# First batch of an attention + Fourier mixing + feed-forward kernel: mirrored columns folded by matmuls, sum and difference accumulated on TensorE, last value products in two steps

## The chip, the cores and the metric

One core of one Trainium2 chip. The metric is the device time of one execution in microseconds (us). The kernel before took 617.75 us, the median of three runs from 617.31 to 617.80. Every variant was timed in five rounds against the kernel before on the same chip.

## The reference

Eight batches, each of 448 positions and 12 heads of 64, hence 768 features.

```python
q_n = q / (norm(q) + 1e-6);  k_n = k / (norm(k) + 1e-6)
attn = softmax(q_n @ k_n.T / tau)
x = concat_heads(attn @ v)                        # [8, 448, 768]
u = x + real(fft(fft(x, axis=1), axis=2))         # mixing over positions, then features
un = (u - mean(u)) / sqrt(var(u) + 1e-6)
out = u + relu(un @ w_ch1) @ w_ch2                # 768 -> 3072 -> 768
```

The kernel does the real part of the two-dimensional transform as cosine and sine tables multiplied on TensorE. Symmetry halves the work: rows k and -k share the products P = C X C and Q = S X S, and one output is P + Q, its mirror P - Q.

## The kernel before

A small scheduler in Python orders the instructions of five engines by estimated durations and priorities; the order it finds is fixed in the program. So any change to batch 0 also reorders what comes after. The parts that matter:

```python
# filler matmuls, put in to keep TensorE's clock up in the head (cut)
n = int(0.75 * (op.start - t - 0.1) / 0.036)
if bank and n > 0:
    new = Op(("pe",), make(bank[0], n), (0.036 * n,), 0, "warm")
# the 24 weight pieces, all on GpSimd's queue; each waits for the piece three before it
for i in range(24):
    ...
    prev.append(P.add("pool", fn, 0.8, 9, nm, writes=[nm], dma=(nm, 16), after=[prev[-3]], serve=2.1))
self.w = prev[3:]
# loads of q and k: those of the third batch (b == 2) wait for the 8th piece of the second matrix
gate = [self.w[19]] if b == 2 else []
# loads of v, also on GpSimd's queue: those of the second batch wait for the 12th piece of the first
gate = [self.loads[3]] if b == 0 else [self.w[11]] if b == 1 else []
# fold: mirrored columns added and subtracted on VectorE into G, then the sequence step fs
return v.tensor_tensor(gp(G[:], ...), gp(F[:], ...), gp(F[:], [[fs_, 2], [384, 2], [-1, n]], ...), o)
...
r = pe.matmul(o, G[0:k, eo, 2 * s + t, ...], self.CSs[0:k, t, s, :], start=(t == 0), stop=(t == 1))
# feature step fd: the cosine product into one bank, the sine product into the next
r = pe.matmul(PS[:, bk + s, m0:m1], self.Tt[0:k, o0:o0 + 128], self.CSd[0:k, d, s, m0:m1], ...)
# ScalarE copies one product out; VectorE makes sum and difference; then the adds into U
P.add("act", lambda a, ...: a.activation(SN[2], PS[:, bank + 1, 0:NL], ACTF.Copy), ...)
for sg, o in ((0, AluOp.add), (1, AluOp.subtract)):
    P.add("dve", lambda v, ...: v.tensor_tensor(SN[sg], PS[:, bank, 0:NL], SN[2], o), ...)
```

## Time and profile before

| | kernel before |
|---|---|
| time, median of 3 | 617.75 us |
| span of the profiled run | 616.0 us |
| TensorE busy | 591.1 us, 96% |
| GpSimd busy | 96.3 us, 16% |
| first feed-forward matmul (line 1000) | 55.96 us |
| first matmul of the second layer (line 1022) | 103.29 us |

Up to 55.96 us is the "head", in which the first batch's attention and transform run while TensorE has nothing of its own to do. From 103.29 us to the end TensorE is busy for 507.4 of 512.7 us. The prediction shows the windows, the chain of waits and GpSimd's timeline.

### The profile page before, as it was taken

Reading aid. Unit: us, or ns where it says so; the run is one execution under the profiler, and the core shown is the slowest. Engines: PE = TensorE matmul, PEld = TensorE weight load, DVE = VectorE, ACT = ScalarE, POOL = GpSimd, SP = SyncE. Lnnn points to the kernel's source line nnn. Section 1 sums busy time; section 2 is a strip of 40 time slices with the busy share of each in tenths; the row PEclk is TensorE's granted clock in tenths of the full one; section 3 lists DMA queues with packets and bytes.
Section 4 is the critical chain, followed back from the end, with each engine's and each line's share of the span. In section 5 each row is a group of like instructions: output and inputs, shape, how many; then the busy total and the mean of one; then the engine's idle time right before and its main releaser. Section 6 shows DMA issues by size and latency. Waiting matters only on the chain.

```text
span 616.0 us, 13590 instructions
## 1 busy us (share of the span) xinstructions
PE 591.1 (96%) x5604; PEld 384.7 (62%) x5621; DVE 389.0 (63%) x896; ACT 346.5 (56%) x690; POOL 96.3 (16%) x125
## 2 busy tenths in 40 slices
PE   4788999999999999999999999999999999999998
PEld 3567777667866666655566676566556766654464
DVE  7887987797778677877788669667643670010011
ACT  7784797247873688347745856685576125104300
POOL 8721512010004102010030130003000010010010
PEclk8899999999999999999999999999999999999999
DMA  7999998889339536973196393716720140010001
GB/s 186 120 213 217 159 181 115 95 153 183 76 72 189 122 78 94 131 168 78 30 142 132 95 173 67 162 53 104 58 40 2 53 102 1 27 39 13 1 27 77
DMA packets 187629, 62.02 MB, mean 101 GB/s; under 512 B 166704, under 2 KB 185264, under 8 KB 187568
## 3 DMA queue, kind: packets, MB, share of 16 engines
q1 hardware_dynamic: 129648, 38.35, 32.4%
q0 software_dynamic: 57920, 22.81, 28.8%
q8 instruction: 44, 0.72, 0.5%
q14 instruction: 17, 0.14, 0.1%
HBM read 51.90 MB, written 11.01 MB: 102 GB/s over the span
## 4 chain that ended last, share of the span: by engine, by line
PE 87%; DVE 6%; ACT 2%; POOL 2%; issue 2%; DMA 1%; POOLq 0%; DVEq 0%; ACTq 0%
PE PS L1000 34%; PE PS L1022 34%; PE PS L782 5%; PE PS L751 5%; PE PS L779 2%; PE PS L847 2%; PE PS L882 2%; ACT E L733 2%; DVE U L903 1%; DMA VB<-in_v_dram 1%; DVE ST L930 1%; PE PS L763 1%; PE PS L764 1%; PE PS L1097 1%; DVE OUTB L1031 0%
## 5 line engine op out<-in xcount | busy, mean ns | idle before, releaser
L1000 PE MATMUL PS<-UNT,W1b 128*128 128x256 bf16 (+3 forms) x1424 | 230.6, 315 | 3.4 <-issue 1.3
L1022 PE MATMUL PS<-W2b,hT 128*128 128x384 bf16 (+2 forms) x1343 | 229.7, 326 | 0.1
L1000 PEld LDWEIGHTS PS<-UNT,W1b 128*128 128x128 bf16 x1440 | 129.2, 98 | 87.2 <-ACT hT L1009 3.0
L1022 PEld LDWEIGHTS PS<-W2b,hT 128*128 128x128 bf16 x1344 | 128.8, 98 | 81.9 <-issue 2.6
L733 ACT ACTIVATE E<-PS 128x900 bf16<-128x900 f32 (+1 forms) x192 | 150.0, 826 | 42.6 <-PE PS L751 35.1
L1009 ACT ACTIVATE hT<-PS 128x384 bf16<-128x384 f32 (+3 forms) x170 | 81.0, 477 | 94.7 <-PE PS L1000 93.2
L1031 DVE TENSOR_TENSOR OUTB<-PS,U 128x384 f32<-128x384 f32 (+2 forms) x56 | 31.2, 557 | 116.1 <-PE PS L1022 115.2
L1052 POOL DMA_INDIRECT out_dram<-OUTB,IDX x20 | 22.0, 1099 | 328.2 <-DVE OUTB L1031 188.8
L668 DVE TENSOR_REDUCE SS<-QH 128x6 f32<-128x384 f32 x84 | 45.4, 541 | 14.0 <-ACT QH L666 13.8
L1010 DVE TENSOR_SCALAR hT<-PS 128x256 bf16<-128x256 f32 (+3 forms) x70 | 35.3, 505 | 27.6 <-PE PS L1000 26.4
L782 PE MATMUL PS<-VB,E 128*128 128x65 bf16 x1152 | 51.2, 193 | 0.0
L782 PEld LDWEIGHTS PS<-VB,E 128*128 128x128 bf16 x1152 | 47.7, 97 | 1.7
L666 ACT ACTIVATE QH<-STG 128x384 f32<-128x384 f32 x84 | 43.6, 519 | 7.2 <-DVE SS L668 4.3
L713 POOL DMA_DIRECT2D VB<-in_v_dram x24 | 25.3, 1063 | 128.7 <-PE PS L782 127.8
L751 PE MATMUL PS<-QT,KT 64*128 64x225 bf16 x576 | 43.1, 262 | 2.0 <-ACT E L733 1.7
L779 PE MATMUL PS<-VZ,E 128*128 128x130 bf16 x192 | 42.3, 220 | 1.5 <-DMA VB<-in_v_dram 1.2
L903 DVE TENSOR_TENSOR U<-SQT,X 128x384 bf16<-128x384 f32 (+3 forms) x80 | 40.8, 551 | 0.8
L675 DVE TENSOR_TENSOR QH<-STG,RN 128x768 bf16<-128x768 f32 x42 | 39.7, 950 | 0.5
L796 DVE TENSOR_TENSOR X<-PS,RD 128x512 bf16<-128x512 f32 x48 | 33.2, 691 | 1.5
L751 PEld LDWEIGHTS PS<-QT,KT 64*128 64x128 bf16 x576 | 21.3, 94 | 20.0 <-ACT E L733 8.7
L794 DVE RECIPROCAL RD<-PS 128x8 f32<-128x8 f32 x48 | 9.9, 206 | 32.2 <-PE PS L782 32.0
L857 ACT ACTIVATE Tt<-PS 128x900 bf16<-128x900 f32 (+2 forms) x15 | 13.4, 893 | 28.1 <-PE PS L847 28.1
(117 smaller groups left out, 485.4 us busy)
## 6 DMA issues: line engine op xcount, KB each, us to landing
STG<-in_q_dram SPq DMA_DIRECT2D x18, 384.0 KB, 5.0
STG<-in_k_dram SPq DMA_DIRECT2D x18, 384.0 KB, 4.0
VB<-in_v_dram POOLq DMA_DIRECT2D x24, 192.0 KB, 6.3
W1b<-in_moe_w_ch_dram POOLq DMA_DIRECT2D x12, 384.0 KB, 8.2
W2b<-in_moe_w_ch_dram POOLq DMA_DIRECT2D x12, 384.0 KB, 6.2
out_dram<-OUTB SPq DMA_DIRECT2D x7, 384.0 KB, 2.4
hT<-in_k_dram SPq DMA_DIRECT2D x2, 576.0 KB, 5.4
hT<-in_q_dram SPq DMA_DIRECT2D x2, 576.0 KB, 6.9
```

The costliest lines, as they stand in the source:

```text
L666: P.add("act", lambda a, sq=sq, src=buf[:, w * x:w * x + w]: a.activation(sq, src, ACTF.Square), t_act(w), pr, f"sq{i}_{b}", reads=bn, wri ...
L668: P.add("dve", lambda v, o=SS[:, i, H // ns * x:H // ns * (x + 1)], sq=sq: v.tensor_reduce(o, sq.rearrange("p (h d) -> p h d", d=DH), AX.X ...
L675: P.add("dve", lambda v, i=i, buf=buf, qh=qh: v.tensor_tensor(v3(qh), v3(buf), RN[:, i, :].unsqueeze(2).to_broadcast((128, H, DH)), AluOp. ...
L733: return a.activation(o, self.PS[:, bk:bk + nc_, 0:SQ2], ACTF.Exp, scale=1.0 / self.tau)
L751: i = pe.matmul(self.PS[:, bk + h, c0:c0 + NK], self.KT[r, jj, kt * 128:(kt + 1) * 128], self.QT[r, jj, cols], start=True, stop=True)
L779: pe.matmul(o, st(6), self.VZ[:, j, :], start=True, stop=False, skip_group_check=True)
L782: r = pe.matmul(o[:, 65 * h:65 * h + 65], st(2 * kt + h), self.VB[:, kt, 2 * j + h, :], start=False, stop=(h == 1 and kt == 2), skip_group ...
L903: return v.tensor_tensor(U[o0:o0 + n, ut, cs].rearrange("p (i e) -> p i e", e=2), src, X[i0:i0 + n, x, cs].rearrange("p (i e) -> p i e", e ...
L1000: r = pe.matmul(self.PS[:, bk, 0:n], self.W1b[:, j, ft * 128:(ft + 1) * 128], unT[:, j, cs], start=(j == 0), stop=(j == NJ - 1))
L1009: return e.activation(self.hT[:, ft, cs], self.PS[:, bk, 0:n], ACTF.Relu)
L1010: return e.tensor_relu(self.hT[:, ft, cs], self.PS[:, bk, 0:n])
L1022: r = pe.matmul(self.PS[:, bk, 0:n], self.hT[:, ft, 128 * i:128 * i + 128], self.W2b[:, ft, c0:c0 + n], start=(ft == 0), stop=(ft == NF - 1))
```

## The change

The intent is to shorten the head. Four things are done to batch 0 only: the last head pair's value products run in two steps; mirrored columns of the first of two blocks are no longer folded on VectorE but multiplied against a mirrored table, as twice as many matmuls (with that, the copy of this block's result, Tt, goes to ScalarE alone); P + Q and P - Q are accumulated on TensorE, the latter with a negated sine table; and fillers come as 8 per 0.6 us in place of one long block. Two negated tables are made by two new GpSimd instructions.

```diff
@@ fill
-                n = int(0.75 * (op.start - t - 0.1) / 0.036)
-                if bank and n > 0:
-                    new = Op(("pe",), make(bank[0], n), (0.036 * n,), 0, "warm")
+                for x in range(int((op.start - t) / 0.6)) if bank else ():
+                    at = t + 0.6 * x
+                    new = Op(("pe",), make(bank[0], 8), (0.288,), 0, "warm")
@@ sequence table, negated, for the fold
+            P.add("pool", lambda g: g.tensor_scalar(self.CSn, self.CSs[:], -1.0, None, AluOp.mult), 1.4, 30, "sinn", ...)
@@ value products
+            split = b == 0 and pos == 5
+            for qp, part in ((0, "m"), (1, "m"), (0, "t"), (1, "t")) if split else ((0, "tm"), (1, "tm")):
@@ fold
+        direct = b == 0 and dj in (0, 2)
...
+                    if direct:
+                        for x, (o0, tab) in enumerate(((0, self.CSs), (257, self.CSs if eo == s else self.CSn))):
+                            for t in range(2):
+                                r = pe.matmul(o, gp(F[0:k], [[1, 128]], (4 * eo + 2 * s + t) * FP + o0), tab[0:k, t, s, :], ...)
@@ fft
+        SP = self.STG[:, 3, :].bitcast(BF)[:, 0:2 * NL].rearrange("p (d c) -> p d c", d=2)
+        if b == 0:
+            P.add("pool", lambda g: g.tensor_scalar(SP, self.CSd[:, :, 1, :], -1.0, None, AluOp.mult), 1.2, pr, "sinp", reads=["CSd"], writes=["STG3"])
...
+                            tab = self.CSd[0:k, d, s, m0:m1] if b or s == 0 or sums[0] == 0 else SP[0:k, d, m0:m1]
-            P.add("act", lambda a, tile=tile: a.activation(SN[2], PS[:, self.bank(tile) + 1, 0:NL], ACTF.Copy),
+            if b:
+              P.add("act", lambda a, tile=tile: a.activation(SN[2], PS[:, self.bank(tile) + 1, 0:NL], ACTF.Copy),
-            for sg, o in ((0, AluOp.add), (1, AluOp.subtract)):
+            for sg, o in ((0, AluOp.add), (1, AluOp.subtract)) if b else ():
```

## The prediction

> **What bounds the kernel now.** I read the page's busy row first: TensorE is busy 591.1 of 616.0 us, so only stretches in which it waits can shrink. Then the windows, to find them:
>
> ```profile
> core 0: us, PE busy (x) PEld busy (x) DVE busy (x) ACT busy (x) POOL busy (x), PEclk, DMA share, GB/s
> 12.10:18.90 6.80, 5.72 (x53) 4.43 (x54) 6.09 (x16) 5.20 (x12) 6.44 (x7) 0.50 1.28 82
> 56.00:64.00 8.00, 7.56 (x109) 6.04 (x110) 7.88 (x17) 5.15 (x20) 3.43 (x5) 1.00 1.30 194
> 64.00:80.00 16.00, 14.55 (x159) 10.98 (x159) 14.62 (x37) 13.20 (x30) 6.65 (x9) 1.00 1.39 163
> 80.00:185.00 105.00, 103.97 (x1123) 76.39 (x1121) 82.59 (x203) 69.10 (x151) 10.14 (x13) 1.00 0.70 123
> 185.00:616.00 431.00, 426.03 (x3436) 259.10 (x3451) 240.08 (x550) 219.43 (x430) 44.98 (x48) 1.00 0.49 80
> ```
>
> From 64 us on TensorE idles 1.45 + 1.03 + 4.97 = 7.5 us of 552. The change touches only the first batch, which is the head: up to 55.96 us, where the first real feed-forward matmul starts. Whatever moves that start moves what follows, as far as TensorE then stays full. So the next view is the chain of waits through the head's end:
>
> ```profile
> 40.83 0.18 PE PS L782 x6
> 41.01 0.65 PE PS L1097 x23
> 41.66 0.79 PE PS L847 x8
> 42.45 2.02 PE PS L1097 x70
> 44.47 2.04 issue
> 46.51 0.46 PE PS L1097 x10
> 46.97 0.81 PE PS L847 x8
> 47.80 0.63 DVE Tt L858
> 48.49 0.86 PE PS L882 x8
> ```
>
> L847 is the sequence Fourier step (fs), L882 the feature step (fd), L1097 filler matmuls that only keep the clock up. The 80 fillers between the two L847 groups are one block without a semaphore in it, yet they stop for 2.04 us after 70. Nothing the profile shows releases them. The vector engine had finished the data at 45.59 us, so the second L847 group was late by some 1.3 us through filler alone. After L882 come ScalarE's copy of one product (0.49), VectorE's sum and difference (4 x 0.55 us), the additions into U, statistics (2 x 0.51), normalisation at 54.23, transposes at 54.75, and the first feed-forward matmul.
>
> A third engine matters, which the chain does not show: GpSimd, whose timeline is a row of waits for weight transfers.
>
> ```profile
> 44.80 0.82 POOL L470 DMA_DIRECT2D W1b<-in_moe_w_ch_dram  x1 [5.24 <-DMA W1b<-in_moe_w_ch_dram]
> 49.29 0.82 POOL L470 DMA_DIRECT2D W1b<-in_moe_w_ch_dram  x1 [3.68 <-DMA W1b<-in_moe_w_ch_dram]
> 53.44 0.82 POOL L470 DMA_DIRECT2D W1b<-in_moe_w_ch_dram  x1 [3.33 <-DMA W1b<-in_moe_w_ch_dram]
> ```
>
> Twelve such issues stand in order; each waits for the piece three before it. These three are the 10th, 11th and 12th. The 11th waits for the 8th piece, which lands at about 49.2 us.
>
> [...] the DMA record has a 16 KiB instruction packet at 44.16 and another at 50.96 us, and fillers stop at 44.47 and again (1.29 us) at 52.1, 127 matmuls later. [...] The 12.10:18.90 row above, at 0.50, follows a 2.6 us gap. [...]
>
> **The change, part by part.**
>
> 1. Last pair's products in two steps. The 22 products that need only early exponentials run before the tail ones. In the chain the block occupied 39.90 to 41.01; I expect some 0.5 us earlier, less 0.18 us for the second reciprocal and about 0.1 for the split X product.
>
> 2. Mirrored columns by matmul. VectorE loses the two L834 instructions of 508 elements (0.77 us for both) and the copy Tt of 900 columns (1.10 us; it goes to ScalarE, after its table load ends at 44.04, so done by 45.0). TensorE gets 8 more 225-column matmuls at 0.81/8 = 0.10, that is 0.8 us, in a gap. Saving on the path: about 1.5 us.
>
> 3. Fillers: 439 before the first feed-forward matmul become 168, about 540 instructions fewer[...]. The 2.04 us stop should go; worth the 1.3 us above.
>
> By 1 to 3 the fd step could start at about 45.9 us instead of 48.49.
>
> 4. Sum and difference on TensorE: 32 matmuls instead of 16 (0.86 us per 8). Removed: two ScalarE copies (0.98) and four VectorE operations (2.2 us). On the path to the first normalised tile, copy + two of the four = 0.49 + 0.56 + 0.48 = 1.5 us go, 0.7 to 0.9 come. Without anything else the feed-forward would start near 52.0 us, 4.0 earlier.
>
> 5. But the difference needs a negated sine table, made by a new GpSimd instruction of 770 elements. I compared the two kernels' instruction orders: it stands behind the 11th weight issue, which still waits for the 8th piece. The transfers were started long before and nothing in the change speeds them. So: issue at 49.29, done at 50.11, then the table, for which I take the 0.85 us of the other 770-element GpSimd instruction (L435): 51.0. Four of the first tile's eight difference matmuls read it, and the semaphore is in front of all eight; TensorE is in order, so everything behind waits too. From 51.1: 8 matmuls 0.86 -> 51.96; second half of the first U tile 0.56, statistics 1.03, aggregate 0.21 -> 53.76, against 53.41 before. The two adds for the next tile (1.0) stand ahead of the normalisation, so that goes from 54.23 to 54.8. This is +0.55 us at full clock.
>
> 6. TensorE idles from about 46.7 to 51.1, 4.4 us without a filler, since the fillers stand behind the blocked step. [...] 8 matmuls of 193 columns cost some 0.6 us more, the transposes 0.3 more (0.82 against 0.49 in the cold and warm L611 groups), and the first feed-forward groups perhaps 0.5. The start then moves to some 57.2, +1.2 us.
>
> 7. Given back: VectorE does 2.2 us less after the step, so tiles two and three are ready at -0.4 to +0.5 us against before. VectorE is full there (7.88 of 8.00, then 14.62 of 16.00), and TensorE has 1.45 us of slack between 64 and 80, so only about half of the later start reaches the end: +0.6 us.
>
> Sum: all of the 4 us is hidden behind a transfer, and 617.75 + 0.6 = 618.35. I say 618.2, for the chance that the table comes in time.
>
> **Rivals.**
>
> A. The table isn't late: the 8th piece lands earlier, or the order inside the engine is looser than I think. For it: the intent, and that only one place in the order is in the way. Against it: 3.68 us of wait in the trace, and a DMA share of 1.26 to 1.33 right through 42 to 56 us. Result 613.8. I give it 15%.
>
> B. The stall as above, but the half clock lasts into the feed-forward[...]. A pair of 12 matmuls, 0.88 us now, would be 1.3, so the start of the stream loses another 1.2 us or more. [...] Result 619.5 to 620.5, 25%.
>
> C. The order of all later instructions is new (the scheduler redid batches 1 to 7), and only 7.5 us of idle is left there. A better or worse packing could be worth 1 to 2 us either way. Nothing in the profile tells the sign.
>
> D. Stall at full clock with the VectorE saving counting in full: 617.2 to 617.8.
>
> **Range and chances.** Centre 618.2. The low end, 614.5, takes in most of A; the high end, 620.6, takes in B with C against it. 2% is 12.4 us; the whole head between the last products and the feed-forward is 15 us and most of that remains, so faster or slower by that much needs a surprise: 0.01 each, 0.98 within.
>
> **What would show it.** In the changed profile: the negating GpSimd instruction starts at 50.1 to 50.3 us, just after the 11th weight issue; TensorE's group of difference matmuls waits for GpSimd some 4 us; a half-clock stretch of 3.4 or 6.8 us begins near 50; no 2 us "issue" wait between the two fs groups; the first feed-forward matmul starts at 56.5 to 57.5. I'm wrong if that matmul starts before 54 (A), if the table is made before the 11th issue, or if the time after its start changes by over 2 us (C).

Cut from it are the statements on how instructions are fetched, on when the clock falls and returns and on how GpSimd's queue works, where no trace of this case shows them. No term of the sum is cut: it came to 617.75 + 0.6 = 618.35, put at 618.2. What its steps rest on:

- Step 3: that fewer fillers remove the stop (1.3 us) was my estimate; in `before_fill` below it did go. The trace shows the instruction transfer at 44.16 us and the stop at 44.47 us; no run isolates the cause, and `fix_oldfill` below, with the old fillers, has no such stop between the two sequence groups.
- Step 5: that what stands behind the difference matmuls waits too is shown by the changed kernel: TensorE runs nothing for 5.43 us, with its fillers behind them in the order.
- Step 6: the half clock was expected because 0.50 followed a gap of 2.60 us in the kernel before, and this gap was to be 4.4 us. The 0.6 us is an estimate; the L611 ratio, 0.82 to 0.49, on 0.86 us gives 0.58. The 0.5 us is a guess from no row and isn't in the 57.2. Fillers do keep the clock: 1.00 from 50 to 54 us in `warm_stall` below, 0.50 without.
- Rival B: 1.3 us for a pair and 1.2 us for the stretch are my estimates. A stretch of 6.80 us was in the kernel before; one of 3.41 us came later, in `v_mid_g16`.

## More of the kernel before

The columns are line, engine, operation, output and input with their shapes, count, then total and mean duration (us, ns), then the idle time before.

```profile
L695 POOL TENSOR_SCALAR CSs<-CSs 1x225 bf16<-1x225 bf16 x2 | 1.5, 774 | 0.2 <-POOL U L404 0.2
...
L435 POOL TENSOR_SCALAR UNT<-U 128x770 f32<-128x770 f32 x1 | 0.9, 854 | 0.1
```

GpSimd takes nearly as long for 225 bf16 elements in a row as for 770 f32 elements.

## The result, and the profile after

The changed kernel took 621.48 us (four runs, 620.94 to 621.97) against 617.77 us (four runs, 617.31 to 618.76). All outputs are right. The ratio is 1.0058, 95% interval 1.004 to 1.0075: slower by 0.6%, above the top of the predicted range (620.6). A ratio here is the mean time of one kernel's fast runs over that of the other's in the same rounds, so it isn't quite the ratio of the medians.

GpSimd's timeline of the changed kernel, at the place of the three issues that the prediction shows (start, duration, then what the idle time before waited for):

```profile
49.69 0.82 POOL L472 DMA_DIRECT2D W1b<-in_moe_w_ch_dram  x1 [2.52 <-DMA W1b<-in_moe_w_ch_dram]
50.58 2.14 POOL L900 TENSOR_SCALAR STG<-CSd 128x770 bf16<-128x770 bf16 x1
53.90 0.86 POOL L472 DMA_DIRECT2D W1b<-in_moe_w_ch_dram  x1 [1.18 <-DMA W1b<-in_moe_w_ch_dram]
```

The negated table (line 900) stands just behind the 11th weight issue, as the instruction order said. It takes 2.14 us, not 0.85. TensorE's timeline shows who waits for it:

```profile
46.51 0.84 PE L916 MATMUL PS<-CSd,Tt 128*128 128x193 bf16 x8 [0.58 <-DVE Tt L888]
52.78 0.51 PE L916 MATMUL PS<-STG,Tt 128*128 128x193 bf16 x2 [5.43 <-POOL STG L900]
```

The eight sum matmuls run at 46.51 us, two microseconds earlier than the feature step before (48.49). The first difference matmul then waits 5.43 us for the table. The chain of waits, in order of time, now runs through a transfer and GpSimd, where before it ran through TensorE's fillers:

```profile
38.06 11.34 DMA W1b<-in_moe_w_ch_dram
...
49.69 0.82 POOL W1b L472
...
50.58 2.15 POOL STG L900
...
52.78 4.06 PE PS L916 x24
56.84 1.24 PE PS L1138 x24
58.08 0.65 PE PS L991 x6
...
58.76 0.57 DVE UNT L999
...
59.39 0.84 PE PS L1041 x12
```

Read it backwards: the feed-forward (line 1041) starts at 59.39 us; the transposes (991) and 24 fillers (1138) come before it (their input, F, was ready at 57.42 us, so the fillers ahead of them in the order held them for about half a microsecond); the 24 feature matmuls take 4.06 us, 0.17 us each where the kernel before took 0.11 (0.86 for 8); they wait for the table, the table for the issue, the issue for a weight piece that was under way since 38.06 us. The slowness of the matmuls is the clock. The windows (stretch, length, busy time of TensorE, its weight loads, VectorE, ScalarE and GpSimd, then granted clock, DMA share and GB/s):

```profile
49.20:59.45 10.25, 6.42 (x63) 6.03 (x64) 4.22 (x10) 2.04 (x4) 4.53 (x4) 0.50 1.31 219
50.00:54.00 4.00, 1.22 (x8) 1.15 (x9) 0.00 (x0) 0.00 (x0) 2.75 (x3) 0.50 1.26 238
```

The clock is at half from 49.20 to 59.45 us. The second row also says that VectorE did nothing at all in the four microseconds around the table, so the 2.14 us aren't a conflict with VectorE. The groups view of the changed kernel has both new tables:

```profile
L700 POOL TENSOR_SCALAR hT<-CSs 128x900 bf16<-128x900 bf16 x1 | 2.5, 2472 | 0.1
...
L900 POOL TENSOR_SCALAR STG<-CSd 128x770 bf16<-128x770 bf16 x1 | 2.1, 2144 | 0.1
```

With the 225-element row above (774 ns), the slope is (2144 - 774) / 545 = 2.51 ns and (2472 - 774) / 675 = 2.52 ns an element: a straight line that the page of the kernel before had one point of.

Four landmarks of each trace carry the rest. Times are us from the start of the span, read from TensorE's timeline.

| kernel | first feed-forward matmul | first value product of the second batch | start of the second layer | end |
|---|---|---|---|---|
| before | 55.96 | 80.88 | 103.29 | 615.99 |
| changed | 59.39 | 81.91 | 107.69 | 620.16 |

The feed-forward starts 3.43 us later and the end is 4.17 us later. So the late start wasn't absorbed: the stretch behind it even grew by 0.74 us (560.03 to 560.77).

### The profile page after: what moved, and what is told of

Its sections match the earlier page's. It is cut to its first block, busy times and chain, and to the rows that moved or that the text cites. A ratio compares the mean times of both kernels' runs of the same rounds, so it can differ in the third digit from the quotient of the medians.

```text
span 620.2 us, 13115 instructions
## 1 busy us (share of the span) xinstructions
PE 590.1 (95%) x5374; PEld 381.9 (62%) x5374; DVE 390.6 (63%) x898; ACT 343.1 (55%) x682; POOL 100.7 (16%) x128
## 4 chain that ended last, share of the span: by engine, by line
PE 89%; DMA 4%; POOL 3%; ACT 2%; issue 1%; DVE 1%; POOLq 0%; DVEq 0%; ACTq 0%
PE PS L1041 36%; PE PS L1063 35%; PE PS L754 5%; PE PS L791 5%; DMA W1b<-in_moe_w_ch_dram 3%; PE PS L916 2%; PE PS L876 2%; PE PS L785 2%; DMA VB<-in_v_dram 1%; ACT E L736 1%; POOL W1b L472 1%; PE PS L767 1%; PE PS L766 1%; POOL hT L700 0%; POOL VB L716 0%
## 5 line engine op out<-in xcount | busy, mean ns | idle before, releaser
L1041 PE MATMUL PS<-UNT,W1b 128*128 128x256 bf16 (+3 forms) x1440 | 234.0, 316 | 1.5 <-DVE UNT L999 0.6
L1050 ACT ACTIVATE hT<-PS 128x384 bf16<-128x384 f32 (+3 forms) x168 | 79.4, 473 | 96.8 <-PE PS L1041 95.6
L1051 DVE TENSOR_SCALAR hT<-PS 128x256 bf16<-128x256 f32 (+3 forms) x72 | 37.3, 518 | 29.4 <-PE PS L1041 27.9
L944 DVE TENSOR_TENSOR U<-SQT,X 128x384 bf16<-128x384 f32 (+3 forms) x70 | 36.3, 552 | 0.7
L809 DVE TENSOR_TENSOR X<-PS,RD 128x512 bf16<-128x512 f32 (+1 forms) x49 | 33.2, 679 | 1.4
L975 ACT ACTIVATE RS<-MV,cst 128x1 f32<-128x1 f32 x28 | 8.2, 292 | 39.1 <-DVE MV L973 38.7
L971 DVE BATCH_NORM_STATS2 ST<-U 128x6 f32<-128x384 bf16 x56 | 28.4, 536 | 0.1
```

Of the source, the lines that this page charges most:

```text
L944: return v.tensor_tensor(U[o0:o0 + n, ut, cs].rearrange("p (i e) -> p i e", e=2), src, X[i0:i0 + n, x, cs].rearrange("p (i e) -> p i e", e ...
L1041: r = pe.matmul(self.PS[:, bk, 0:n], self.W1b[:, j, ft * 128:(ft + 1) * 128], unT[:, j, cs], start=(j == 0), stop=(j == NJ - 1))
L1050: return e.activation(self.hT[:, ft, cs], self.PS[:, bk, 0:n], ACTF.Relu)
L1051: return e.tensor_relu(self.hT[:, ft, cs], self.PS[:, bk, 0:n])
```

## The experiments

Theories after the first look. T1: the late table is the whole cause; make it early and the 4 us that the change was meant to give appear. T2: the late table is the first of several waits on the weight stream, and the next one takes its place. T3: the new order of later batches costs as much by itself. Ratios are always to the kernel before of the same rounds, whose medians were 617.0 to 617.26 us.

### Table made early, and table made by VectorE

`table_early` keeps the instruction on GpSimd but orders it ahead of the 10th weight issue (and keeps the 10th to 12th issues in order):

```diff
+                self.w[9].order = (self.sinp,)
+                self.w[10].order = (self.w[9],)
+                self.w[11].order = (self.w[10],)
```

> The changed kernel with one thing moved: the negated sine table stays on GpSimd but stands ahead of the 10th weight issue instead of behind the 11th. Orders on TensorE, VectorE and ScalarE are identical. Theory (the late table holds the difference matmuls): the table runs about 43.8 to 45.9 us, the difference matmuls no longer wait, the first feed-forward matmul starts near 52.5 us (59.4 in the changed kernel), and the time falls to 615 to 616 us, less than the full 7 us because the last weight pieces, which land near 63 us, begin to be waited for. Rival 1 (the loss comes from the new order of the later batches or from the extra matmuls): the time stays at 620 to 622. Rival 2 (the half clock alone costs it): also better, but only if the clock stays full; by itself this run cannot tell it from the theory.

Measured: 619.15 us, ratio 1.0031 (1.0009 to 1.0054). `table_dve` gives the same instruction to VectorE:

```diff
-            P.add("pool", lambda g: g.tensor_scalar(SP, self.CSd[:, :, 1, :], -1.0, None, AluOp.mult), 1.2, pr, "sinp", ...)
+            P.add("dve", lambda g: g.tensor_scalar(SP, self.CSd[:, :, 1, :], -1.0, None, AluOp.mult), 0.35, pr, "sinp", ...)
```

> The changed kernel with the negated sine table made by VectorE in its gap near 44.7 us instead of by GpSimd. Theory: as the run with the table moved ahead, within 0.5 us: 615 to 616 us, feed-forward start near 52.5 us. The weight issues now run without the table's 2.1 us between them, which should not matter. If engine speed mattered rather than place, this would be clearly better than the moved table.

Measured: 619.34 us, 1.0028 (1.0004 to 1.0052).

| kernel | first feed-forward matmul | first value product of the second batch | start of the second layer | end |
|---|---|---|---|---|
| table_early | 53.90 | 78.10 | 103.86 | 616.35 |
| table_dve | 53.75 | 79.25 | 105.34 | 617.83 |

Both start the feed-forward two microseconds before the old kernel does, as T1 wants, and both are still slower than it. T1 falls. TensorE's timeline of `table_early`, then of `table_dve`, shows where the gain goes:

```profile
78.10 0.22 PE L785 MATMUL PS<-VZ,E 128*128 128x130 bf16 x1 [1.56 <-DMA VZ<-in_v_dram]
```

```profile
79.25 0.22 PE L785 MATMUL PS<-VZ,E 128*128 128x130 bf16 x1 [2.93 <-DMA VZ<-in_v_dram]
```

Line 785 is the first value product of the second batch. Its values VZ are issued on GpSimd's queue behind weight pieces and land at 78 to 79 us however early the feed-forward began. That is T2: a floor made of the weight stream.

### The table made twice

`table_twice` repeats the GpSimd instruction, so that everything behind it comes later by one table.

```diff
             P.add("pool", lambda g: g.tensor_scalar(SP, ...), 1.2, pr, "sinp", reads=["CSd"], writes=["STG3"])
+            P.add("pool", lambda g: g.tensor_scalar(SP, ...), 1.2, pr, "sinp2", reads=["CSd"], writes=["STG3"])
```

> The changed kernel with the GpSimd table instruction issued twice in the same place. Theory: the stall grows by the instruction's own 2.15 us and all of it reaches the end: 621.5 + 2.1 = 623.6 us. If only half of a later start reaches the end, as the prediction had it: 622.5. If the table were not on the path: 621.5.

Measured: 624.06 us, 1.0103 (1.0078 to 1.0129). GpSimd's timeline:

```profile
50.66 2.15 POOL L900 TENSOR_SCALAR STG<-CSd 128x770 bf16<-128x770 bf16 x1
52.88 2.15 POOL L901 TENSOR_SCALAR STG<-CSd 128x770 bf16<-128x770 bf16 x1
```

The feed-forward starts at 61.70 us, 2.31 later than in the changed kernel, and the span ends at 622.49 us, 2.33 later. Here a later start passes to the end one to one. Six traces of the changed order that start between 58.30 and 61.70 us (this one, the changed kernel twice, and `warm_stall`, `warm_again` and `after_v_early` below) all have 560.57 to 560.80 us from there to the end. This contradicts the prediction's step 7, which let half be absorbed; no trace has a start between 55 and 58 us in the new order, where the predicted 57.2 lies.

### TensorE kept busy through the stall

`warm_stall` puts 32 matmuls of 385 columns, which nobody reads, between the sum and the difference matmuls, so that the clock stays up.

```diff
+                def keep(pe):
+                    for _ in range(32):
+                        r = pe.matmul(PS[:, 7, 0:NL], self.ID[:], self.CSd[:, 0, 0, :], start=True, stop=True, ...)
+                if b == 0 and kt == 0 and sg:
+                    P.add("pe", keep, 0.0, pr + 1, "keep", reads=["CSd"], tiles=(wt,), acquire=wt, after=[self.fd_ops[-1]])
```

> The changed kernel with 32 matmuls of 385 columns (about 5.2 us) between the first sum and the difference, so TensorE keeps its clock while it waits for the table; they write an unused PSUM bank. Orders are otherwise identical. Theory: the stall stays (difference matmuls start near 52.8 us), the 24 Fourier matmuls then take about 2.1 us instead of 4.1, feed-forward start near 58.0 us instead of 59.4, time about 620.1. Rival 2 (the half clock is the main cost): 618 or less.

Measured: 621.13 us, 1.0055 (1.0032 to 1.0078). Its weight piece happened to land 0.8 us later in the profiled run, so it was run again beside the changed kernel on one chip.

> The run with the kept clock once more, beside the changed kernel on one chip. Theory (the half clock costs 1.3 us of start, as 5.30 us from the table's end to the feed-forward against 6.66 says, and the 8th weight piece landing 0.8 us later in that one trace was chance): 1.0 to 1.4 us faster than the changed kernel. Rival (the added matmuls themselves delay the weight piece or the rest): no difference.

> The changed kernel as it is, for a same-chip base of the other three: 621 to 622 us.

Measured there: `warm_again` 620.71 us, 1.0062 (1.0049 to 1.0075); `after_again`, the changed kernel itself, 621.24 us, 1.0077 (1.0063 to 1.0091). TensorE's timeline of `warm_stall`, then its window over the same four microseconds as above:

```profile
47.40 5.39 PE L923 MATMUL PS<-CSd,ID 128*128 128x385 bf16 x32
53.62 0.34 PE L916 MATMUL PS<-STG,Tt 128*128 128x193 bf16 x2 [0.82 <-POOL STG L900]
```

```profile
50.00:54.00 4.00, 3.18 (x23) 1.86 (x21) 0.00 (x0) 0.00 (x0) 2.96 (x2) 1.00 1.26 237
```

The clock stays at 1.00, and two difference matmuls take 0.34 us in place of 0.51. From the table's end to the feed-forward passes 5.30 us (5.32 in `warm_again`), against 6.66 in the changed kernel and 5.93 in `after_again`, where the half clock ended some 3.4 us sooner (at about 56.0 us: the clock is 0.50 from 50 to 54 us, 0.75 from 54 to 58). So the half clock costs 0.6 to 1.4 us of the start, and it differs from run to run. In the timed runs the gain was 0.5 us, with intervals that overlap, less than the 1.0 to 1.4 that I expected. It is the smaller part of the loss.

### The new filler rule on the old kernel

`before_fill` is the kernel before with only the new rule for fillers (the first part of the diff).

> The kernel before with the new filler rule alone (168 fillers instead of 439; all other orders identical). Theory: the 2.04 us stop[...] between the two sequence Fourier groups goes, the second group starts near 45.8 instead of 46.97 us, and the time falls by 1.0 to 1.3 us, to about 616.6. Rival: the fillers were needed for the clock, a half-clock stretch appears and the time rises to 618 or more.

Measured: 618.87 us, 1.0026 (1.0013 to 1.0039): a miss, it got slower. The stop among the fillers did go, and the feature step starts at 47.01 us in place of 48.49. (The trace has 256 fillers before the feed-forward, not the 168 that I expected.) In this trace, that of the fastest run (617.60), the feed-forward starts 1.20 us earlier than in the kernel before (54.76), the second layer only 0.21 us earlier (103.08). The windows of this run show a half-clock stretch where the kernel before has none at this place:

```profile
51.80:58.60 6.80, 6.01 (x67) 5.67 (x68) 6.23 (x15) 3.42 (x9) 1.52 (x2) 0.50 1.33 209
```

That is where the early start goes: the first 108 feed-forward matmuls take 9.29 us, in the kernel before 7.93. A thin filler isn't the only way to such a stretch: two traces with the old fillers have one too (the kernel before from 12.10 to 18.90 us at 0.50, `before_v_early` from 55.5 us, 0.83 over 50 to 60). Why the slower timed runs, up to 619.52, lost two more microseconds isn't shown, since the profiled run was not one of them.

### Parts of the change taken back, with the table on VectorE

Three kernels start from `table_dve`: `fix_oldfill` has the old filler rule, `fix_nosplit` sets `split = False` and takes the last value products in one step, `fix_nodirect` sets `direct = False`.

> The changed kernel with the table on VectorE, but with the old filler rule. Theory: a stop[...] comes back somewhere between 40 and 52 us and costs 1 to 1.5 us against the run with the table on VectorE.

> The changed kernel with the table on VectorE, without the two steps for the last pair's value products. Theory: the split brought about 0.2 us (0.5 earlier products less 0.28 for the second reciprocal and the split product), so within 0.4 us of the run with the table on VectorE.

> The changed kernel with the table on VectorE, but with the mirrored columns folded by VectorE again in place of the extra matmuls. The first evacuation stays on ScalarE. Theory: two VectorE instructions of 0.39 us each come back ahead of the last products, about 0.8 to 1.0 us slower than the run with the table on VectorE, less where the weights are the limit.

| kernel | time | ratio | first feed-forward matmul | second batch's first value product |
|---|---|---|---|---|
| table_dve | 619.34 | 1.0028 (1.0004 to 1.0052) | 53.75 | 79.25 |
| fix_oldfill | 619.82 | 1.0042 (1.0029 to 1.0055) | 52.06 | 78.18 |
| fix_nosplit | 618.55 | 1.0028 (1.0016 to 1.0041) | 52.36 | 77.80 |
| fix_nodirect | 619.00 | 1.0033 (1.0020 to 1.0046) | 54.88 | 78.70 |

The times can't tell the parts apart: the values' landing decides, whatever the head does. The starts say a little: without the direct fold the head is about a microsecond longer than in `table_dve`; both had the clock at half from 22 to 29 us (0.66 over 20 to 30 us in `table_dve`, 0.85 over 18.9 to 42 us in `fix_nodirect`). `fix_oldfill` and `fix_nosplit` did not (1.00 over 18.9 to 42 us), so they can't be set against `table_dve`. They can be set against `v_mid_g16` and `v_mid_g17` below, which have the head of `table_dve` and kept their clock up to 52 us (1.00 in every window): these start the feed-forward at 51.85 and 51.74, so the two-step products gain 0.5 to 0.6 us and the old fillers cost 0.2 to 0.3, by one or two traces each.

### The second batch's values moved ahead

If the values are the floor, moving their issue ahead must lift it. `v_early` is `table_dve` with these loads ahead of all pieces of the second matrix, and released by the 9th piece of the first in place of the 12th:

```diff
-            gate = [self.loads[3]] if b == 0 else [self.w[11]] if b == 1 else []
+            gate = [self.loads[3]] if b == 0 else [self.w[8]] if b == 1 else []
+                for v in self.vl[4:8]:
+                    v.order = (self.w[11],)
+                self.w[12].order = (self.vl[7],)
```

`v_early_oldfill` is the same with the old filler rule. `before_v_early` and `after_v_early` are the same edit on the two kernels.

> The run with the table on VectorE, and the second batch's value loads put ahead of the second layer's weight issues on GpSimd. Other orders identical. Theory (with the stall gone, the first value product of the second batch waits for its values, which stand behind weight issues in the GpSimd queue): that product starts at 75 to 76.5 us instead of 79.3 and without a DMA wait, the second layer starts 25.8 us after it, and the time falls 2 to 4 us below the run with the table on VectorE: 615.5 to 617. Rival (the new order of the second batch is itself slow whatever the values do): no gain, 619.

> As the run with early value loads, with the old filler rule. The old rule kept TensorE at full clock between 18 and 75 us where the thin one let it drop in 22 to 29 us in some traces. Theory: the start of the feed-forward is steadier and now counts, so 0 to 1.5 us faster than with the thin filler[...].

> The kernel before with the second batch's value loads put early in the same way. Theory: there they landed in time, so nothing changes: 616.9 to 617.8. If the early values help by themselves, the gain of the early-values run isn't due to the removed stall.

> The changed kernel, table still late on GpSimd, with the second batch's value loads put early. Theory: its late start covers the value loads, so no gain: 621 to 622. If the values were the cause of the loss all along: 618 or less.

| kernel | time | ratio | second batch's first value product | start of the second layer |
|---|---|---|---|---|
| v_early | 627.24 | 1.0118 (1.0070 to 1.0166) | 75.72 | 112.93 |
| v_early_oldfill | 625.90 | 1.0119 (1.0087 to 1.0152) | 77.00 | 113.53 |
| before_v_early | 619.86 | 1.0032 (1.0014 to 1.0050) | 81.95 | 104.36 |
| after_v_early | 621.82 | 1.0069 (1.0051 to 1.0087) | 81.72 | 107.49 |

`after_v_early` did what was expected: nothing, since the table holds its start. `v_early` missed badly. Its value product came at 75.72 us without a wait for values, 3.5 us sooner than in `table_dve`, and yet the second layer starts 7.6 us later. (Its runs lie in two places, 618.47 once and 626.75 to 627.93; the ratio uses those counted as fast.) The old kernel gets slower by the edit too, where I expected nothing; its trace has the second batch 1.1 us later. There the normalisation on VectorE (line 939) takes 0.81 us where it took 0.47, while GpSimd issues the moved loads; then the clock is at half from 55.5 to 58.9 us (0.83 over 50 to 60), and the first 108 feed-forward matmuls take 8.76 us in place of 7.93. What made the normalisation slow was not tested.

A milder move, `v_mid`, shows the cause of the miss. It puts the values ahead of only two pieces, the 4th and 5th of the second matrix:

```diff
+                for v in self.vl[4:8]:
+                    v.order = (self.w[14],)
+                self.w[15].order = (self.vl[7],)
+                self.w[16].order = (self.w[15],)
```

> The run with the table on VectorE, and the second batch's value loads moved only past two weight issues of the second layer (the 4th and 5th), not past five as in the early-values run. Other orders identical. Theory (with the stall gone, the values' landing near 78 to 79 us is the floor; in the early-values run that floor went but the delayed weights delayed the third batch's loads): the first value product of the second batch starts at 75.5 to 77 us, the second layer 25.8 us later, 2 to 3 us faster than the table-on-VectorE run of the same chip, so 616 to 617.5. Rival (any room given to the values is taken from transfers that are needed as early): no gain or a loss.

Measured: 623.50 us, 1.0090 (1.0052 to 1.0129), runs from 617.62 to 626.08. The chain of waits of `v_mid`:

```profile
78.38 6.60 DMA W2b<-in_moe_w_ch_dram
...
84.99 0.60 SPq L662
...
85.63 10.48 DMA STG<-in_k_dram
...
96.20 0.52 ACT QH L668
96.72 0.82 ACT E L736
...
97.58 0.56 PE PS L754 x4
```

and ScalarE's timeline of the same run:

```profile
96.20 0.52 ACT L668 ACTIVATE QH<-STG 128x384 f32<-128x384 f32 x1 [6.99 <-DMA STG<-in_k_dram]
```

A piece of the second matrix lands at 85.0 us. That releases the loads of the third batch (line 662), which take until 96.1 us. ScalarE's squaring of them (line 668) waits 6.99 us, with the second batch's exponentials (line 736, at 96.72 us) behind it in ScalarE's order, and TensorE's scores (line 754, at 97.58 us) wait for those. So the next floor is the third batch's loads, held by the 8th piece of the second matrix, and a piece moved back moves them back. `v_early` shows the same chain, with a wait of 8.94 us at the squaring.

### Both floors lifted

`v_mid_g16` and `v_mid_g17` are `v_mid` with the third batch's loads released by the 5th or the 6th piece in place of the 8th:

```diff
-        gate = [self.w[19]] if b == 2 else []
+        gate = [self.w[16]] if b == 2 else []      # v_mid_g16;  self.w[17] in v_mid_g17
```

> The run with the values moved past two weight issues, and the third batch's loads released by the 5th weight piece of the second layer in place of the 8th. Orders on all engines identical. Theory (in that run ScalarE waited 7.0 us for the third batch's first loads, which are released by the 8th piece): the wait goes, the second layer starts near 101 to 102 us, and the time falls to 614.5 to 616, below the kernel before. Rival (the transfers as a whole are full, so what one gets another lacks): a wait for another transfer appears, the weights of the second layer most likely, and the time stays at 617 to 622.

> As the run released by the 5th piece, with the 6th: between it and the run with the values moved alone. Theory: if the 5th is early enough to hurt the weights, this is the better of the two; else it is 0.5 to 2 us slower than it.

Measured: 615.59 us, 0.9970 (0.9956 to 0.9983), and 615.49 us, 0.9969 (0.9956 to 0.9983), with runs within 1 us of one another. This is the expected result, and the first variant that beats the kernel before. TensorE's timeline of `v_mid_g16` at the first floor, then ScalarE's at the second:

```profile
75.46 0.22 PE L785 MATMUL PS<-VZ,E 128*128 128x130 bf16 x1 [0.18 <-DMA VZ<-in_v_dram]
```

```profile
86.03 3.33 ACT L736 ACTIVATE E<-PS 128x900 bf16<-128x900 f32 x4 [0.35 <-PE PS L754]
89.25 0.51 ACT L668 ACTIVATE QH<-STG 128x384 f32<-128x384 f32 x1
89.77 0.92 ACT L736 ACTIVATE E<-PS 128x900 bf16<-128x900 f32 x1
```

The wait for values is 0.18 us, and the squaring follows the exponentials with no wait at all. Landmarks: 51.85, 75.46, 101.22, 613.72 us. The start is 4.11 us before the old kernel's, the end 2.27. Part of the rest is the clock: it is at half from 52.17 to 55.58 us, just after the start. `v_mid_g17` kept it (1.00 from 52 to 64 us); its start is 4.22 us before the old kernel's (51.74) and its end 2.94 (613.05).

The same moves of loads on the old kernel were not run. Its trace leaves them little: between 80.88 and 103.29 us TensorE idles 0.27 us, and neither it nor ScalarE waits for a transfer.

### The repeat on one chip

> The table on VectorE once more, beside the changed kernel on one chip: 2.0 to 2.6 us faster than it, with the first value product of the second batch waiting for its transfer at 78 to 79.5 us.

Measured beside `after_again`: 620.24 us, 1.0061 (1.0048 to 1.0074), 1.0 us faster than the changed kernel where I expected 2.0 to 2.6. In the traces the feed-forward starts at 53.18, 5.34 us earlier, and the span ends 0.94 us earlier. Most of it was lost again at the first floor, where TensorE waited 3.77 us for the values.

## Why the prediction was wrong

The wait and what causes it were forecast rightly. The length of the table, the time from its end to the start, and the share of the late start that is absorbed were not.

**Right.** The table stood just behind the 11th issue (predicted 50.1 to 50.3 us, measured 50.58). TensorE waited for GpSimd, the clock fell to half near 50 us (0.50 from 49.20), and there was no two-microsecond stop among the fillers between the two sequence groups. "About 45.9" for the feature step and "near 52.0" for a feed-forward start without the late table were right where the clock held between 20 us and the feature step: 45.58 to 46.36 and 51.74 to 52.36 in `v_mid_g16`, `v_mid_g17`, `fix_oldfill` and `fix_nosplit`. In six traces with a half-clock stretch between 22 and 34 us (0.85 over 18.9 to 42 us in `table_early` and `table_dve`) the start is 52.59 to 53.90, which the prediction did not foresee. Rival A was rightly thought unlikely.

**Wrong: the 0.85 us in step 5.** I took it from the only GpSimd row with 770 elements and didn't look at its type. That row is f32; the bf16 row of the same operation, 225 elements in 0.77 us, was on the same page. The table took 2.15 us in the chain. (That the type makes the difference isn't shown: other f32 tensor-scalar rows of that page, lines 404 and 440, took 1258 and 1526 ns for 385 elements.) In the start of the feed-forward the sum is: table begins 0.47 us later than I said (50.58, not 50.11), table 1.30 us longer, and from its end to the start 6.66 us where I had 6.24, which is 0.42. Together 2.19, from the predicted 57.2 to the measured 59.39.

**Too short: the half clock in step 6.** It lasted 10.25 us (49.20 to 59.45) where I had named 3.4 or 6.8; in `after_again` it lasted about 6.8. It fell 1.85 us after TensorE stopped at 47.35 us, in the kernel before 2.28 us after (9.82 to 12.10), and returned 6.67 us after work resumed at 52.78 us, in `after_again` about 3.35 us after. Yet it ended with the start of the feed-forward and not inside it, so rival B didn't come true as told. (My own terms, 0.55, 0.6 and 0.3 us on 55.96, make 57.4 and not the 57.2 that I wrote; from there the 0.42 would be 0.2.)

**Wrong: step 7, "only about half of the later start reaches the end".** I argued from VectorE being full and TensorE having slack. `table_twice` shows all of it reaching the end, 2.31 to 2.33. Of the predicted 1.24 us I had let 0.6 through, so that is 0.64 us more; of the measured 3.43 us, halving would have hidden 1.7.

**Rival C, with no sign given.** The stretch behind the start grew by 0.74 us, 0.97 up to the second layer and -0.23 after (0.54 to 0.77 in the six traces named under `table_twice`, against the one of the kernel before). I put it down to the new order of the later instructions, which no run isolates. Which instruction of the order costs it isn't shown; the variants keep 25.75 to 26.1 us from the second batch's first value product to the second layer where nothing stalls, against 22.41 in the old order, and pay less before it (22.52 against 24.92 in the changed kernel).

T3 falls with this as the main cause: the order may cost something, but about a fifth of the loss.

The four terms, the predicted 0.6 among them, give 0.6 + 2.19 + 0.64 + 0.74 = 4.17 us, which is the difference of the spans.

**Where the intended gain went.** I wrote that all of the 4 us was "hidden behind a transfer", and meant one. There are three in a row, all in or behind GpSimd's queue of weight pieces: the 8th piece of the first matrix (through the 11th issue and the table), the second batch's values, and the third batch's loads. Removing the first gave 1 to 2 us and showed the second; removing the second alone gave nothing (`after_v_early`), and the first two without the third were worse than nothing (`v_mid`, `v_early`); with all three removed the changed head is worth 0.3% of the time over the kernel before, and 615.5 against 621.2 to 621.5 us over the changed kernel (not of the same rounds). Open remain the slow runs of `before_fill`, the slow normalisation in `before_v_early`, what decides when the clock falls, and the order's own cost.

## What to carry to other kernels

Take a duration from a row of the same engine, operation and type (0.85 us taken, 2.14 measured), and if there are two candidates on the page, ask why they differ. An instruction put into a queue of transfer issues takes over the waits ahead of it (TensorE waited 5.43 us for the table), and so does a load that such an issue releases (ScalarE waited 6.99 us for the third batch in `v_mid`). A later start may reach the end in full (2.31 us of start, 2.33 of end in `table_twice`) while an earlier start stops at the next transfer's landing (78.10 us in `table_early`), so before shortening a head, list the landings that follow it and what releases each.
